# Seven block products for the last matrix product of an attention and two-layer expert kernel

## The chip, the cores and the metric

The kernel runs on one core of one Trainium2 chip. A core has TensorE (matmuls; PE in the profile, its weight loads PEld), VectorE (DVE), ScalarE (ACT), GpSimd (POOL) and SyncE (SP), which here issues all DMAs. Matmuls write to PSUM, eight banks of 512 fp32 numbers on each of 128 partitions; GpSimd can't read it. The metric is the device time of one execution in microseconds, lower is better. Inputs and outputs are fp32.

## The reference

```python
# attention with a small memory: q, k, v (8, 8, 576, 64), phi (8, 8, 576, 32)
a = softmax(phi, axis=2)
k_m = einsum('bhsm,bhsd->bhmd', a, k); v_m = einsum('bhsm,bhsd->bhmd', a, v)
attn = softmax(q @ k_m.T / sqrt(64)) @ v_m
x = attn.transpose(0, 2, 1, 3).reshape(4608, 512)
# first layer, d_ff 768
h = maximum(maximum(x @ w1, x @ w2), x @ w3)
x = h @ w_out                                   # 768 -> 512
# second layer, d_ff 1536
gate = 1 / (1 + exp(-(x @ w_gate)))             # 512 -> 1536
out = (gate * (x @ w_val)) @ w_out              # 1536 -> 512
```

The change concerns the last line alone: `gg = gate * val`, 4608 x 1536, times the second `w_out`, 1536 x 512.

## The kernel before

The program is written with a tile framework. It traces the instructions in the order of the Python code; a scheduler with a model of the engines then orders each engine's queue, and sets the waits. It may move instructions past one another, on TensorE and on SP as well, unless an instruction is pinned with `tc.keep_in_program_order`. Tiles come from pools: a tag with `bufs=n` has n buffers, and a new tile waits for the last reader of the tile that had its buffer.

**Precision.** A product of fp32 matrices is made of three matmuls in the type fp32r. `w_split` (L133) makes two parts of a matrix: ACT casts it to the high part, then GpSimd or VectorE subtracts that from the whole to get the low part (`sub`, L72). `PASSES` (L333) lists low x high, high x low, high x high, summed in PSUM.

**First half** (to about 559 us): attention, and the first layer in four passes of 1152 tokens (`h_step` L362, `x2_step` L389). Its output x goes to HBM as `x2s`. In the last pass, beside `x2_step`, the first operands of the second half are made.

**Second half.** The 4608 tokens are cut into five chunks (`SUPER`), each of two halves of 512, 512, 512, 384 and 384 tokens. In each chunk, six rounds j = 0..5 take 256 of the 1536 columns of d_ff: the two blocks of 128 columns j and j+6. A round of one chunk:

- *Up products.* x (two halves of tokens by two halves of the 512 inputs) times the gate weights (v = 0) and the value weights (v = 1) is a 2 x 2 block product. It is made in seven block products (Winograd's form of Strassen's method) for eight: seven sums of blocks of x (`XA`, made by `x_sums` and `x_split` once a chunk), seven of the weights (`TB`, made in the first chunk by `t_make`, kept in HBM as `tbs` and loaded by `t_load` from then on). `ORDER` = 1, 6, 2, 7, 5, 4, 3 is the order of the products. `up` (L734) makes one for one v: `product` (L691), six matmuls of 512 columns (384 in the small chunks), 14 ups a round.
- *Blocks.* `up` then joins the products to blocks (token half c, column block h). Products accumulate in the PSUM tags px, pz and pv, two banks each; ACT copies product 1 (L746), VectorE makes the sums u (L749). `block_done` (L712) makes a block: for v = 0 the sum (VectorE, L719) and the sigmoid (ACT, L721), for v = 1 the sum (L726) and the product with the sigmoid (L727, or L729 straight from PSUM). Then gg is split: cast on ACT (L731), difference on GpSimd (L732, which the profile shows under the helper's line 73). Block (0,0) comes after product 2, (1,1) after 5, (1,0) after 4, (0,1) after 3.
- *Down products.* `down` (L759) multiplies a row block of 128 tokens with the two blocks of `w_out` of this round: six matmuls of 512 columns into a bank of tag po (two banks). The accumulators `acc` lie in SBUF: ACT copies the first round's sum (L774), VectorE adds the others (L777). Down products of round j stand between the up products of round j+1, from the third up on. After the last round of a chunk the rows go to `out`.

`w_out` is split by `wo_make` in the first chunk, kept as `wos`, and loaded by `wo_load` later. Its tiles and those of TB share 11 buffers (`NQ`). The gate, value and w_out weights come as tiles `tw` by `tw_load` from `wbf`, those of round 0 into the 11 buffers, the later ones into three buffers of the pool `b2`, which takes the place of the first half's pool `low`.

When the next chunk's x is due (`x_load` in the fifth round), GpSimd makes its sums and ACT and GpSimd its seven splits in the sixth round.

Of the kernel before, what the change touches and what calls it, by code (L numbers as in the profile page):

```python
# [1 line left out]

# [16 lines left out]
def attn_moe_kernel(  # L19
# [443 lines left out]
    def t_make(j, pr):  # L463
# [13 lines left out]
        TB[0, j, pr] = kept(src, tbs[j, pr - 1], "tb", vec if pr in (2, 5) else pool)  # L477

    def wo_make(j):
        for h, i in enumerate((j, j + NJ)):  # L480
            WO[0, j, h] = kept(TW[j, 2][:, h], wos[i], "wo2", vec if h else pool)
# [5 lines left out]
    def wo_load(sc, j):  # L487
        for h in range(2):
            t = WO[sc, j, h] = q4_tile("wo2")
            dma(f32(t), wos[j + h * NJ])  # L490
# [220 lines left out]

    def block_done(sc, j, v, c, h, ps, other):  # L712
# [18 lines left out]
        act.copy(t[:, 0, :half], gf)  # L731
        sub(pool, t[:, 1, :half], gf, f32(t[:, 0, :half]))  # L732

    def up(sc, j, pr, v):  # L734
# [12 lines left out]
        elif pr in (6, 7):  # L747
            u = E["u", pr, v] = small(f"u{pr}", 2)[:, :half]
            vec.tensor_tensor(out=u, in0=ps[:, :half], in1=E["p1", v], op=ALU.add)  # L749
# [130 lines left out]
```

## Time and profile before

| | us |
|---|---|
| median of 3 runs | 1387.36 (1386.55 to 1387.68) |
| the profiled execution | 1387.49 |
| its span, first to last instruction | 1385.4 |
| mean granted clock of TensorE | 0.988 |
| down matmuls (L765), 1296 | 327.8 busy |
| evictions of the down products on VectorE (L777), 180 | 124.3 busy |
| differences of gg on GpSimd, 120 | 143.4 busy |

The page gives busy time, share and number of instructions of each engine, then the span in slices (a digit is a tenth; PEclk is the clock granted to TensorE). The view by stretches has one row for each stretch of time: its length, then busy us and number of instructions of PE, PEld, DVE, ACT and POOL, the granted clock, the DMA share and GB/s. The view by order in time has start, length, engine, line, operation, tiles, shape and count of merged instructions; brackets name idle time before them and what ended it. The view by line and shape has count, busy us, mean ns, idle us before and what ended it. The name px stands for all buffers of that tag.

### The profile page before, as it was taken

Reading aid. Unit: us, or ns where it says so; the run is one execution under the profiler, and the core shown is the slowest. Engines: PE = TensorE matmul, PEld = TensorE weight load, DVE = VectorE, ACT = ScalarE, POOL = GpSimd, SP = SyncE. Lnnn points to the kernel's source line nnn. Section 1 sums busy time; section 2 is a strip of 40 time slices with the busy share of each in tenths; the row PEclk is TensorE's granted clock in tenths of the full one; section 3 lists DMA queues with packets and bytes.
Section 4 is the critical chain, followed back from the end, with each engine's and each line's share of the span. In section 5 each row is a group of like instructions: output and inputs, shape, how many; then the busy total and the mean of one; then the engine's idle time right before and its main releaser. Section 6 shows DMA issues by size and latency. Waiting matters only on the chain.

```text
span 1385.4 us, 22143 instructions
## 1 busy us (share of the span) xinstructions
PE 1337.5 (97%) x7864; PEld 1183.9 (85%) x7864; DVE 863.1 (62%) x1533; ACT 576.3 (42%) x1220; POOL 514.6 (37%) x454
## 2 busy tenths in 40 slices
PE   6688999999999999999999999999999999999998
PEld 3578899999999989788888888888888899999997
DVE  5999759966975895566765344453445444554454
ACT  5687546645654664453343321233222322233221
POOL 2775422422331227553586111461112712161111
PEclk9899999999999999999999999999999999999999
DMA  9588757776757745965556544465454666566651
GB/s 314 178 273 304 265 171 262 238 236 225 235 165 261 240 131 170 336 243 198 198 198 228 183 166 153 167 205 190 159 178 167 210 228 222 198 227 237 211 202 72
DMA packets 112269, 292.43 MB, mean 211 GB/s; under 512 B 12576, under 2 KB 28960, under 8 KB 112160
## 3 DMA queue, kind: packets, MB, share of 16 engines
q1 hardware_dynamic: 112160, 291.03, 61.9%
q8 instruction: 62, 1.02, 0.3%
q14 instruction: 47, 0.39, 0.1%
HBM read 224.92 MB, written 66.06 MB: 210 GB/s over the span
## 4 chain that ended last, share of the span: by engine, by line
PE 79%; DVE 10%; DMA 4%; issue 2%; ACT 2%; POOL 1%; SPq 1%; DVEq 0%; ACTq 0%; POOLq 0%
PE po L765 21%; PE px L698 15%; PE pv L698 10%; PE pz L698 10%; PE ps L393 9%; PE ps L370 8%; DVE g L73 2%; PE ps L343 2%; PE ps L209 1%; PE ps L246 1%; DVE ca L129 1%; DVE ca L128 1%; DMA raw<-wb_dram 1%; DVE hm L382 1%; DVE hm L381 1%
## 5 line engine op out<-in xcount | busy, mean ns | idle before, releaser
L765 PE MATMUL po<-wo,gg 128*128 128x512 f32 x1296 | 327.8, 392 | 1.0 <-POOL gg L73 1.0
L73 POOL TENSOR_TENSOR gg<-gf,gg 128x512 fp32r<-128x512 f32 (+1 forms) x120 | 143.4, 1195 | 469.1 <-ACT gg L731 426.3
L765 PEld LDWEIGHTS po<-wo,gg 128*128 128x128 f32 x1296 | 242.4, 188 | 49.5 <-POOL gg L73 1.3
L370 PE MATMUL ps<-attn,g 128*128 128x288 f32 x1728 | 258.7, 302 | 21.0 <-DVE g L73 11.0
L370 PEld LDWEIGHTS ps<-attn,g 128*128 128x128 f32 x1728 | 244.7, 193 | 31.8 <-DVE hm L381 8.7
L698 PE MATMUL px<-xa,tb 128*128 128x512 f32 (+1 forms) x1080 | 244.1, 368 | 1.6 <-DVE gf L729 1.1
L777 DVE TENSOR_TENSOR acc<-po,acc 128x512 f32<-128x512 f32 x180 | 124.3, 691 | 176.0 <-PE po L765 175.8
L698 PEld LDWEIGHTS px<-xa,tb 128*128 128x128 f32 x1080 | 198.0, 188 | 30.4 <-DVE gf L729 1.6
L698 PE MATMUL pz<-xa,tb 128*128 128x512 f32 (+1 forms) x720 | 169.5, 368 | 1.8 <-DVE u L749 1.8
L698 PE MATMUL pv<-xa,tb 128*128 128x512 f32 (+1 forms) x720 | 170.4, 369 | 0.0
L73 POOL TENSOR_TENSOR h<-hm,h 128x288 fp32r<-128x288 f32 x96 | 82.7, 864 | 211.8 <-DVE h L70 111.3
L393 PE MATMUL ps<-h,wo 128*128 128x288 f32 x1152 | 158.5, 296 | 0.0
L393 PEld LDWEIGHTS ps<-h,wo 128*128 128x128 f32 x1152 | 154.3, 188 | 2.8 <-issue 2.6
L698 PEld LDWEIGHTS pz<-xa,tb 128*128 128x128 f32 x720 | 132.2, 188 | 20.9 <-issue 2.2
L698 PEld LDWEIGHTS pv<-xa,tb 128*128 128x128 f32 x720 | 132.8, 189 | 18.1
L731 ACT CAST gg<-gf 128x512 fp32r<-128x512 f32 (+1 forms) x120 | 69.4, 578 | 176.3 <-DVE gf L727 130.5
L749 DVE TENSOR_TENSOR u<-pz,p 128x512 f32<-128x512 f32 (+1 forms) x120 | 76.2, 635 | 97.9 <-PE pz L698 93.4
L73 DVE TENSOR_TENSOR g<-ps,g 64x384 fp32r<-64x384 f32 x180 | 99.4, 552 | 31.8 <-ACT g L357 28.8
L721 ACT ACTIVATE sg<-sg 128x512 f32<-128x512 f32 (+1 forms) x90 | 53.1, 590 | 145.4 <-DVE sg L719 145.1
L357 ACT CAST g<-ps 64x384 fp32r<-64x384 f32 x192 | 90.7, 473 | 36.4 <-DVE g L73 22.4
L73 POOL TENSOR_TENSOR xa<-xf,xa 128x512 fp32r<-128x512 f32 (+1 forms) x64 | 78.8, 1252 | 21.6 <-ACT xa L134 21.6
L727 DVE TENSOR_TENSOR gf<-gf,sg 128x512 f32<-128x512 f32 (+1 forms) x90 | 70.9, 788 | 10.9 <-ACT sg L721 1.3
(92 smaller groups left out, 1394.4 us busy)
## 6 DMA issues: line engine op xcount, KB each, us to landing
tb<-tbs SPq DMA_DIRECT2D x168, 512.0 KB, 3.8
wx<-wxs SPq DMA_DIRECT2D x72, 384.0 KB, 3.9
wo<-wos SPq DMA_DIRECT2D x48, 512.0 KB, 5.4
tbs<-tb SPq DMA_DIRECT2D x42, 512.0 KB, 2.9
raw<-wb_dram SPq DMA_DIRECT2D x48, 384.0 KB, 3.5
kv<-kvm_dram SPq DMA_DIRECT2D x48, 256.0 KB, 5.3
raw<-wx_dram SPq DMA_DIRECT2D x24, 384.0 KB, 3.8
wxs<-wx SPq DMA_DIRECT2D x24, 384.0 KB, 4.4
```

The costliest lines, as they stand in the source:

```text
L73: eng.tensor_tensor(out=o, in0=a, in1=b, op=ALU.subtract)
L343: pe.matmul(ps[:, :384], lhsT=vt[:, x, 2 * e:2 * e + 2].rearrange("p a m -> p (a m)"), rhs=w[:, y], start=(n == 0), stop=(n == 2),)
L357: act.copy(t[r, 0], ps[r, :384])
L370: pe.matmul(ps[w][:, :U], lhsT=G[b, j, g][:, x, 128 * w:128 * w + 128], rhs=at[:, y, hf * U:hf * U + U], start=(n == 0), stop=(n == 5),)
L393: pe.matmul(ps[:, :U], lhsT=wo1_t[:, x, (d * J + j) * 128:(d * J + j) * 128 + 128], rhs=H[u, j][:, y], start=(n == 0), stop=(n == 3 * J - 1),)
L698: pe.matmul(ps[:, :half], lhsT=w[:, a, o:o + 128], rhs=x[:, k, c, :half], start=(first and n == 0), stop=(n == 5), skip_group_check=not first,
L721: act.activation(out=sg, in_=src, func=AF.Sigmoid)
L727: vec.tensor_tensor(out=gf, in0=gf, in1=sg, op=ALU.mult)
L731: act.copy(t[:, 0, :half], gf)
L749: vec.tensor_tensor(out=u, in0=ps[:, :half], in1=E["p1", v], op=ALU.add)
L765: pe.matmul(ps, lhsT=GG[sc, j, c, h][:, x, 128 * m:128 * m + 128], rhs=WO[sc, j, h][:, y], start=(n == 0), stop=(n == 5),)
L777: vec.tensor_tensor(out=t, in0=ps, in1=t, op=ALU.add)
```

## The change

From the second chunk on, the product of gg and `w_out` is made in seven block products too. gg of a round is 2 x 2 blocks (c, h); the round's part of `w_out` is 2 x 2 blocks (h, half of the 512 outputs). The seven left sides are gg's blocks 1: (0,0), 2: (0,1), 4: (1,1) and sums 3, 5, 6, 7, made on VectorE in `block_done`; each is split as a block was, so there are seven splits a round for four. The seven right sides are made in the first chunk, which itself still uses eight products (`down0`, the old `down`), by `wo_make`, six steps a round, and kept in `wos`.

`down` makes a product for two row blocks at a time: six matmuls of 256 columns (three where a half has a third row block alone) into one bank, evicted at once. The seven products are accumulated each for itself over the six rounds; after the sixth `add` joins them to the four output blocks, on GpSimd and VectorE, all on VectorE in the last chunk. A down product follows each up product, from the first on. Products 1 and 4 come first, then those that are made late. `InOrder` pins every matmul of the second half behind the one traced before it.

```diff
+    class InOrder:
+
+        def __init__(self, eng):
+            self.eng = eng
+
+        def __getattr__(self, name):
+            fn = getattr(self.eng, name)
+            return lambda *a, **k: tc.keep_in_program_order(fn(*a, **k))
...
-    wos = tc.dram_tile([NI, 128, 2, DM], F32, name="wos")
+    wos = tc.dram_tile([NI // 2, 7, 128, 2, DM // 2], F32, name="wos")
...
-    NQ = 11
+    NQ = 7
     ORDER = (1, 6, 2, 7, 5, 4, 3)
+    DORDER = (1, 4, 6, 7, 5, 2, 3)
+    LORDER = (1, 6, 7, 5, 4, 2, 3)
+    HD = DM // 2
...
         for h, i in enumerate((j, j + NJ)):
-            t = TW[j, h] = tile()
+            t = TW[j, h] = b1.tile([128, 2, DM], F32, tag="tw", name="tw", bufs=2)
             dma(t.rearrange("p h c -> p (h c)"), wbf[i, :, 0:2 * DM])
-        t = TW[j, 2] = tile()
+
+    def wv_load(j):
+        t = TW[j, 2] = b2.tile([128, 2, DM], F32, tag="wv", name="wv", bufs=1)
...
+    def wo_load(sc, j, n):
+
+        order = dorder(sc, j)[2 * n:2 * n + 2]
+        t = wo_tile().rearrange("p a (h d) -> p h a d", h=2)
+        for h, pr in enumerate(order):
+            WO[sc, j, pr] = t[:, h]
+            dma(f32(t[:, h]), wos[j, pr - 1])
...
+    pe = InOrder(nc.tensor)
...
+    def gg_split(sc, j, pr, x):
+        half = SUPER[sc][1]
+        t = GG[sc, j, pr] = b2.tile([128, 2, 512], F32R, tag="gg", name="gg", bufs=8)
+        w_split(x, t[:, 0, :half], t[:, 1, :half])
...
+        elif (c, h) == (1, 0):
+            A11, A22 = F[0, 0], F[1, 1]
+            vec.tensor_tensor(out=A22, in0=gf, in1=A22, op=ALU.add)
+            sub(vec, gf, A11, gf)
+            sub(vec, A11, A22, A11)
+            for pr, x in ((6, A11), (7, gf), (5, A22)):
+                gg_split(sc, j, pr, x)
+        else:
+            gg_split(sc, j, 2, gf)
+            sub(vec, gf, gf, F[0, 0])
+            gg_split(sc, j, 3, gf)
...
+    def add(sc, x, y):
+        n = SUPER[sc][1] // 128
+        a, b = ACC[sc, x][:, :n], ACC[sc, y][:, :n]
+        (vec if x in (3, 5) or sc == LAST[0] else pool).tensor_tensor(out=a, in0=a, in1=b, op=ALU.add)
+
+    BLOCK = {2: (0, 0), 3: (0, 1), 4: (1, 0), 5: (1, 1)}
...
+    BEFORE = {1: ((2, 1),), 7: ((7, 6), (4, 7)), 6: ((6, 1),), 5: ((3, 5), (3, 6), (5, 7))}
+
+    def bank_of(sc, j, n):
+        tag = "po" if (sc, j) != LAST else ("po", "px", "pz", "pv")[n // 2 % 4]
+        return psB.tile([128, 512], F32, tag=tag, name=tag, bufs=2)
...
+    def down(sc, j, pr, q):
+        n = SUPER[sc][1] // 128
+        m0, m1 = 2 * q, min(2 * q + 2, n)
+        at = 2 * dorder(sc, j).index(pr) + q
+        ps = bank_of(sc, j, at).rearrange("p (m d) -> p m d", m=2)
+        for m in range(m0, m1):
+            for k, (x, y) in enumerate(PASSES):
+                pe.matmul(
+                    ps[:, m - m0],
+                    lhsT=GG[sc, j, pr][:, x, 128 * m:128 * m + 128],
+                    rhs=WO[sc, j, pr][:, y],
+                    start=(k == 0), stop=(k == 2),
+                )
+        if j == 0 and q == 0:
+            ACC[sc, pr] = acc_tile()
+        summed(j, ACC[sc, pr][:, m0:m1], ps[:, :m1 - m0])
...
+        if j == NJ - 1:
+            for x, y in BEFORE.get(pr, ()):
+                add(sc, x, y)
...
+        if (sc, j) != LAST and (at % 4 == 3 or at == 13):
+            wo_load(*after(sc, j), at // 4)
...
-                    if slot >= 3 and downs:
-                        down(*downs.pop(0))
+                    if downs and slot >= downs[0][0]:
+                        downs.pop(0)[1]()
...
+                x = [(pr, q) for pr in dorder(sc, j) for q in range(2)]
+                downs = [(n + 1, partial(down, sc, j, *a)) for n, a in enumerate(x)]
```

Other edits that go with it:

- `LORDER` is the order of the last round of all, whose bank comes from all four PSUM tags in turn.
- The sums of the next chunk's x move from the sixth round to the fourth (from the third chunk's x on), and half of the seven splits of x (those of products 6, 7 and 4) have their differences on VectorE, where GpSimd had all.
- The weights `tw` of all rounds lie in two buffers of the pool `b1`, the w_out weights (`wv`) in one buffer of `b2`; `wo_make` of round 0 moves from the end of the first half into the first round. Tiles of TB have the seven buffers alone, `w_out` has four of its own.
- The tile of product 7's sum u takes the buffer of p1; gg has 8 buffers for 6; the accumulators are seven tiles of 1024 numbers for eight of 512; `x2` has a pool of its own.

More of the change, by code (lines that the diff above doesn't have):

```diff
@@ L1 @@
 from contextlib import ExitStack
+from functools import partial
 import concourse.bass as bass
@@ L476, in t_make, with wo_tile, wo_make @@
             src = TD.pop(pr)
[L477 to L481, printed above, removed]
+        TB[0, j, pr] = kept(q4_tile("tb"), src, tbs[j, pr - 1], vec if pr in (2, 5) else pool)
+    def wo_tile():
+        return b2.tile([128, 2, DM], F32R, tag="wo2", name="wo2", bufs=4)
+    def wo_make(j, n):
+        w = TW[j, 2]
+        B11, B12, B21, B22 = w[:, 0, :HD], w[:, 0, HD:], w[:, 1, :HD], w[:, 1, HD:]
+        if n < 2:
+            t = WO[0, j, n] = wo_tile()
+            w_split(w[:, n], t[:, 0], t[:, 1], vec if n else pool)
+            for pr, c in (((1, 0),), ((2, 0), (3, HD)))[n]:
+                dma(wos[j, pr - 1], f32(t[:, :, c:c + HD]))
+            return
+        pr = (6, 7, 5, 4)[n - 2]
+        if pr == 6:
+            sub(vec, B11, B12, B11)
+            TD["w"] = b2.tile([128, HD], F32, tag="wd", name="wd", bufs=1)
+            sub(vec, TD["w"], B22, B11)
+        elif pr == 7:
+            sub(vec, B12, B22, B12)
+        elif pr == 4:
+            sub(vec, TD["w"], B21, TD["w"])
+        x = {5: B11, 7: B12}.get(pr)
+        t = b2.tile([128, 2, HD], F32R, tag="wt", name="wt", bufs=1)
+        kept(t, TD["w"] if x is None else x, wos[j, pr - 1], pool)
     def t_load(sc, j, pr):
@@ L485, in t_load, with dorder @@
         dma(f32(t), tbs[j, pr - 1])
[L487 to L490, printed above, removed]
+    def wo_load(sc, j, n):
[4 more added lines that the diff above has]
+            dma(f32(t[:, h]), wos[j, pr - 1])
+    def dorder(sc, j):
+        return LORDER if (sc, j) == LAST else DORDER
     XA = {}
@@ L653, in attn_moe_kernel @@
                 b1 = tc.alloc_tile_pool(name="b1", bufs=1, side="right", reuse_waits="tile")
+                xo = tc.alloc_tile_pool(name="xo", bufs=1, side="right")
             gens = []
@@ L722, in block_done @@
             return
-        gf = small("gf", 4)[:, :half]
+        gf = F[c, h] = small("gf", 4)[:, :half]
         sg = E.pop(("sg", c, h))
@@ L747, in up @@
         elif pr in (6, 7):
-            u = E["u", pr, v] = small(f"u{pr}", 2)[:, :half]
-            vec.tensor_tensor(out=u, in0=ps[:, :half], in1=E["p1", v], op=ALU.add)
+            p1 = E["p1", v]
+            u = E["u", pr, v] = p1 if pr == 7 else small("u6", 2)[:, :half]
+            vec.tensor_tensor(out=u, in0=ps[:, :half], in1=p1, op=ALU.add)
         elif pr == 2:
@@ L757, in up, with store, acc_tile, summed @@
             block_done(sc, j, v, 0, 1, ps, E["u", 6, v])
-    def down(sc, j, c, m):
-        t0, half = SUPER[sc]
-        ps = psB.tile([128, DM], F32, tag="po", name="po", bufs=2)
+    def add(sc, x, y):
[3 more added lines that the diff above has]
+    BLOCK = {2: (0, 0), 3: (0, 1), 4: (1, 0), 5: (1, 1)}
+    def store(sc, pr, m0, m1):
+        t0, half = SUPER[sc]
+        c, d = BLOCK[pr]
+        r0 = t0 + c * half
+        dma(out[r0 + 128 * m0:r0 + 128 * m1, d * HD:d * HD + HD].rearrange("(m p) d -> p m d", p=128),
+            ACC[sc, pr][:, m0:m1])
+    BEFORE = {1: ((2, 1),), 7: ((7, 6), (4, 7)), 6: ((6, 1),), 5: ((3, 5), (3, 6), (5, 7))}
+    def bank_of(sc, j, n):
+        tag = "po" if (sc, j) != LAST else ("po", "px", "pz", "pv")[n // 2 % 4]
+        return psB.tile([128, 512], F32, tag=tag, name=tag, bufs=2)
+    def acc_tile():
+        return b2.tile([128, 4, HD], F32, tag="acc", name="acc", bufs=7)
+    def summed(j, t, ps):
+        if j == 0:
+            act.copy(t, ps)
+        else:
+            vec.tensor_tensor(out=t, in0=ps, in1=t, op=ALU.add)
+    def down0(sc, j, c, m):
+        half = SUPER[sc][1]
+        ps = bank_of(sc, j, 0)
         n = 0
```

77 lines of the change are left out of this document (45 added, 32 removed).

## The prediction, made before the run

> **What bounds the kernel now.** The page was read first, then busy time by stretches, then the order in time on TensorE.
>
> ```profile
> span 1385.4 us, 22143 instructions
> PE 1337.5 (97%) x7864; PEld 1183.9 (85%) x7864; DVE 863.1 (62%) x1533; ACT 576.3 (42%) x1220; POOL 514.6 (37%) x454
> PEclk9899999999999999999999999999999999999999
> ```
> ```profile
> 559.10:585.60 26.50, 23.07 (x93) 18.03 (x92) 15.22 (x19) 11.58 (x22) 13.62 (x10) 0.94 0.88 323
> ...
> 800.00:900.00 100.00, 100.00 (x441) 82.55 (x440) 48.27 (x73) 22.63 (x38) 25.63 (x20) 1.00 0.46 158
> ...
> 1100.00:1200.00 100.00, 100.00 (x521) 92.76 (x520) 46.14 (x79) 24.38 (x48) 20.74 (x21) 1.00 0.64 221
> ```
>
> In the second half (from 559 us, the part that the change touches) TensorE is busy without a hole, at the full clock, while VectorE is busy for less than half of it (48.27 and 46.14 of 100 us) and the DMA engines for 46 to 64%. Only the first round of it (559 to 586 us) has holes. A busy matmul row is not matmul work at its peak, so the next view is the pitch, from one start to the next:
>
> ```profile
> 914.39 2.88 PE L698 MATMUL px<-xa,tb 128*128 128x512 f32 x12
> 917.11 2.88 PE L698 MATMUL pz<-xa,tb 128*128 128x512 f32 x12
> ...
> 922.09 2.91 PE L765 MATMUL po<-wo,gg 128*128 128x512 f32 x12
> 924.84 1.52 PE L698 MATMUL px<-xa,tb 128*128 128x512 f32 x6
> ```
> ```profile
> 1264.65 2.27 PE L698 MATMUL px<-xa,tb 128*128 128x384 f32 x12
> 1266.75 0.86 PE L698 MATMUL pz<-xa,tb 128*128 128x384 f32 x4
> ```
> ```profile
> 544.74 14.58 PE L393 MATMUL ps<-h,wo 128*128 128x288 f32 x109
> 559.16 2.92 PE L698 MATMUL px<-xa,tb 128*128 128x512 f32 x12
> ```
> ```profile
> 251.67 0.60 PE L195 MATMUL ps<-ident,et 128*128 128x128 f32 x4
> 252.10 0.27 PE L196 MATMUL ps<-ident,et 128*64 128x128 f32 x1
> ```
>
> 512 columns: 2.72 us / 12 = 227 ns in the up products and 2.75 / 12 = 229 ns in the down products (L765). 384 columns: 2.10 / 12 = 175. 288 columns: 14.42 / 109 = 132. Transposes of 128 columns: 0.43 / 4 = 108. Every one loads 128x128 weights of its own. From 288 to 512 columns the pitch grows by 95 ns over 224 columns, 0.42 ns each. So TensorE bounds this half, and what counts there is columns with a small fixed part per matmul.
>
> **The change, part by part.**
>
> *1. Down products.* A round is one value of j, 256 columns of d_ff; a chunk of halves of 512 tokens has 4 row blocks in each half, one of 384 has 3. Now a round has 2 x 4 x 6 = 48 matmuls of 512 columns (36 in the small chunks). After the change it has 7 x 4 x 3 = 84 of 256 (63). No row has 256 columns. The line through 288 and 512 gives 132 - 32 x 0.42 = 119 ns. Bounds: 132 (it can't be dearer than the wider 288) and 108 (transposes with the same weight load). I take 119, next to the 288 row. A large round: 84 x 119 = 10.00 us for 48 x 229 = 10.99. A small one: 7.50 for 8.24. Rounds whose down products run beside the next round's up products: 12 large, 11 small. 12 x 0.99 + 11 x 0.74 = **20.1 us less**. These are 12 x 84 + 11 x 63 = 1701 matmuls, so a pitch of 132 adds 22.1 us and one of 108 takes off 18.7 more.
>
> The Trainium skill (TensorE: Matmul & The Clock Gate, "Back-to-back issue gap") gives N/2.4 + 2.5 ns for a warm matmul alone, 109 ns at 256 columns. By it the sum would be 17 us lower; but it gives 216 ns at 512 columns, where this trace has 227, so the line through the rows stands.
>
> *2. The last round.* Its down products stand alone after the last up product.
>
> ```profile
> 1369.89 2.24 PE L698 MATMUL pv<-xa,tb 128*128 128x384 f32 x12
> ...
> 1373.13 8.53 PE L765 MATMUL po<-wo,gg 128*128 128x512 f32 x36 [1.00 <-POOL gg L73]
> ...
> 1381.69 0.69 DVE L777 TENSOR_TENSOR acc<-po,acc 128x512 f32<-128x512 f32 x1 [0.68 <-PE po L765]
> ```
> ```profile
> L777 DVE TENSOR_TENSOR acc<-po,acc 128x512 f32<-128x512 f32 x180 | 124.3, 691 | 176.0 <-PE po L765 175.8
> ...
> L749 DVE TENSOR_TENSOR u<-pz,p 128x384 f32<-128x384 f32 x48 | 26.7, 556 | 35.2 <-PE pz L698 33.4 <-ACT p L746 1.8
> ```
>
> Now: from the end of the last up product (1369.89 + 2.24 = 1372.1) to the last eviction (1382.4) 10.3 us, set by TensorE. After: 7 evictions of 512 elements at 0.69, 7 of 256, and 7 sums of 768, all on VectorE in the last chunk. From 384 (556 ns) and 512 (691) an element costs 1.05 ns, so 256 take 0.42 us and 768 take 0.96. 7 x 0.69 + 7 x 0.42 + 7 x 0.96 = 14.5 us; with the last block's add, product and difference (3 x 0.56), one eviction left over (0.42) and about 1 us of gaps, 17.6 us. TensorE would need some 9. **VectorE sets the tail: 7.3 us more** (5 to 9).
>
> *3. Work beside TensorE.* Three more casts on ACT, three more differences on POOL, four sums on VectorE and 14 evictions for 8, each round.
>
> ```profile
> L73 POOL TENSOR_TENSOR gg<-gf,gg 128x512 fp32r<-128x512 f32 x72 | 94.7, 1315 | 267.8 <-ACT gg L731 224.9 <-PE po L765 40.9 <-DMA tw<-wbf 1.9
> L731 ACT CAST gg<-gf 128x512 fp32r<-128x512 f32 x72 | 44.8, 622 | 106.2 <-DVE gf L727 75.4 <-DVE gf L729 29.2 <-PE po L765 1.5
> tb<-tbs SPq DMA_DIRECT2D x168, 512.0 KB, 3.8
> ```
>
> POOL: 7 x 1.32 = 9.2 of 29 us; ACT: 1.9 us more; both are hidden, since the first operand that is made late (product 6, after up product 4) is used seven steps of 2.1 us later. Were that cover gone, each would cost up to its 1.9 us. Of DMA, w_out goes from 1.0 to 1.75 MB a round (14 issues for 2 on SP's queue, counting halves); a load has most of a 22 to 29 us round and takes about 4 to land (3.8 for tb), so I cost it at nothing. The queue for tb has 7 buffers for 11, but each load is still issued a round ahead. VectorE: 14 x 0.69 + 10 x 0.69 (reads of PSUM in the blocks) + 0.69 + 7 x 0.69 + about 0.8 of gaps = 22.9 of 29.1 us, 79%. Not the bound in a mean round.
>
> *4. TensorE's order fixed.* A matmul that waits now holds up everything behind it, and evictions are what it can wait for: the down products have two PSUM banks, so a bank must be free 4.15 us after its matmuls ended (two ups of 1.36, two downs of 0.71).
>
> ```profile
> 933.74 0.69 DVE L726 TENSOR_TENSOR gf<-pv,u 128x512 f32<-128x512 f32 x1 [0.21 <-PE pv L698]
> 934.53 0.69 DVE L727 TENSOR_TENSOR gf<-gf,sg 128x512 f32<-128x512 f32 x1
> 935.14 0.68 DVE L719 TENSOR_TENSOR sg<-px,u 128x512 f32<-128x512 f32 x1
> ```
> ```profile
> 704.47 0.69 DVE L726 TENSOR_TENSOR gf<-pv,u 128x512 f32<-128x512 f32 x1 [0.29 <-PE pv L698]
> 705.80 1.31 DVE L73 TENSOR_TENSOR wo<-tw,wo 128x512 fp32r<-128x512 f32 x1 [0.64 <-ACT wo L134]
> 707.03 1.77 DVE L727 TENSOR_TENSOR gf<-gf,sg 128x512 f32<-128x512 f32 x1
> ```
> ```profile
> L727 DVE TENSOR_TENSOR gf<-gf,sg x90: 557/692/1843, 581.4 to 1372.9; 128x512 f32<-128x512 f32 x54, 128x384 f32<-128x384 f32 x36
> ```
>
> After up product 4 VectorE has add, product and three sums in a row. A dependent step takes 0.79 us (933.74 to 934.53), an independent one 0.61. If the eviction traced behind them waits for all: 0.3 + 4 x 0.79 + 0.61 + 0.69 = 4.8 us, counted from the up product's end, where TensorE wants the bank after 4.15: 0.6 us lost, in 16 rounds 10 us. In the round after each of three chunk changes three sums of 1024 elements (1.23 each) come on top, about 3.3 us each time, 10 in all; in the round before, six differences for the next x, 1.5 us each time, 4.5 in all. Together **0 to 25 us**. But the second fence shows an instruction that the program gives later (the w_out difference) put between two dependent ones. Where evictions slip in so, a bank is late by one instruction, within the slack. I take 4.
>
> *5. The entry.*
>
> ```profile
> 570.78 0.62 ACT L134 CAST tb<-tw 128x512 fp32r<-128x512 f32 x1 [8.08 <-DMA tw<-wbf]
> ...
> 585.68 2.88 PE L698 MATMUL px<-xa,tb 128*128 128x512 f32 x12
> ```
>
> The first round takes 585.68 - 559.16 = 26.5 us for 84 x 227 ns = 19.1: 7.4 lost, behind a load of gate weights that ACT waits for. That load now goes to buffers that exist earlier, but w_out's comes in its place, and the order can't bend round a wait. Between 7 less and 4 more; I take 2 less.
>
> Sum: -20.1 + 7.3 + 4 - 2 = -10.8. The profiled execution took 1387.49 us, 2.1 more than its span of 1385.4, and the median is 1387.36, the same within 0.01%. 1387.4 - 10.8 = **1376.6 us**; its own range 1371 to 1382.
>
> **Rivals.**
>
> *VectorE's queue holds up TensorE* (slower). The strict order of part 4 holds: 25 us of stalls for 4, 1387.4 - 20.1 + 7.3 + 25 - 2 = 1397.6. It decides once evictions end more than 4.15 us after their matmuls. For: the fixed order, 79% load, and L727 at 1843 ns where it usually takes 692, which POOL's longer hours make commoner. Against: the slipped instruction. At 13 us of stalls it comes to 1385.6, no difference.
>
> The Trainium skill (SBUF — State Buffer, "Who interferes with whom") says that a VectorE instruction with two SBUF inputs and a GpSimd one that reads SBUF exclude each other for the whole instruction. L727's 1843 ns agrees; the new sums are all of that kind.
>
> *Narrow matmuls don't get cheaper*: 256 columns at 132 ns, as the 288 row. 22.1 us more than forecast: 1398.7. Against: 108 ns was reached with the same weight load.
>
> *All of it comes through*: no stalls and 6 us won at the entry, 1387.4 - 20.1 + 7.3 - 6 = 1368.6. For: TensorE never waits between 600 and 1372 us now.
>
> *Pitch at the lower bound*, 108 ns: 18.7 less than forecast, 1358.
>
> **How the numbers follow.** Forecast 0.50; VectorE's queue 0.16, half-way (no difference) 0.10; narrow matmuls 0.06; all of it 0.15; lower pitch 0.03. A measurement of this kernel tells 0.2% (2.8 us) from no change. Faster: 0.50 + 0.15 + 0.03 = 0.68. Same: 0.10. Slower: 0.22. The range takes in the forecast, half-way, most of "all of it", most of VectorE's queue and the nearer side of the narrow matmuls: 1364 to 1399.
>
> **What would show it.** Step 1: down matmuls at a pitch of 119 ns. Step 2: VectorE without idle time from the last up product on, TensorE done some 8 us earlier than it. Step 4: TensorE's idle time put down to the eviction of po, at most 0.3 us a round. Step 5: the first round of chunk one, 19 to 26 us. A pitch above 130 ns, or 20 us of waits for po, makes the prediction wrong.

## The result, and the profile after

| | before | after |
|---|---|---|
| median of the runs, us | 1387.24 | 1401.90 (1401.55 to 1402.63, 4 runs) |
| ratio, 95% interval | | 1.0111 [1.0099, 1.0123] |
| span of the profiled execution, us | 1385.4 | 1399.9 |
| start of the second half, us | 559.2 | 558.6 |
| chunks 0 to 4, us | 175.1, 180.2, 180.2, 140.1, 137.4 | 182.8, 176.9, 180.7, 144.7, 134.7 |
| last up product to the end of the span, us | 13.2 | 21.6 |

The change makes the kernel 1.1% slower; 1376.6 us had been forecast. A chunk here lasts from the start of its first up product to the start of the next chunk's; round (c, j) is round j of chunk c, cut after every 84 up matmuls (before, the scheduler mixes neighbouring rounds). The page after:

```profile
span 1399.9 us, 24589 instructions
PE 1328.9 (95%) x8620; PEld 1204.9 (86%) x8620; DVE 1048.1 (75%) x1833; ACT 624.4 (45%) x1344; POOL 629.1 (45%) x538
```

TensorE is busy for 8.6 us less than before, yet the span is 14.5 us longer: its work did shrink, but the time around it grew by more. VectorE has 185 us more to do, GpSimd 115. Busy time by rounds of after, (0,2), (2,0), (2,4), (3,0), (3,3) and (4,0), shows where the waits are (columns: length, then PE, PEld, DVE, ACT, POOL, clock, DMA share, GB/s), and below it one round of before:

```profile
615.97:648.47 32.50, 30.84 (x134) 24.62 (x133) 25.71 (x35) 13.28 (x26) 20.75 (x16) 1.00 0.72 251
...
918.25:953.13 34.88, 30.48 (x170) 25.33 (x169) 28.47 (x37) 8.73 (x16) 26.37 (x17) 1.00 0.63 195
1040.63:1069.80 29.17, 29.17 (x170) 25.72 (x169) 21.08 (x33) 7.51 (x13) 9.21 (x7) 1.00 0.60 190
1098.97:1131.14 32.17, 26.72 (x171) 24.88 (x169) 29.47 (x38) 8.06 (x16) 25.12 (x16) 0.97 0.73 224
1177.29:1199.32 22.03, 22.03 (x149) 22.03 (x148) 16.47 (x33) 6.01 (x13) 6.99 (x7) 1.00 0.80 255
1243.67:1268.37 24.70, 23.26 (x150) 21.79 (x148) 20.72 (x36) 6.93 (x15) 16.79 (x13) 1.00 0.76 245
```
```profile
644.15:674.17 30.02, 30.02 (x133) 24.78 (x132) 21.45 (x29) 10.36 (x19) 11.10 (x10) 1.00 0.56 207
```

Rounds (2,4) and (3,3) have no hole: 29.17 us for 30.02 before, and 22.03 for 22.88. That is the gain, 12 x 0.86 + 11 x 0.85 = 19.7 us. Rounds right after a chunk change lose it again: (2,0) lasts 5.7 us more than 29.17; (3,0), which has the small chunk's 84 ups at 173 ns and the large chunk's 84 downs at 118, 24.4 together, loses 7.7. There GpSimd is busy for 26 and 25 us, in a steady round for 9.

```profile
1040.63 1.55 PE L60 MATMUL px<-xa,tb 128*128 128x512 f32 x6
1042.02 0.87 PE L60 MATMUL po<-wo,gg 128*128 128x256 f32 x6
1042.73 1.52 PE L60 MATMUL px<-xa,tb 128*128 128x512 f32 x6
```

In time order on TensorE in (2,4): six matmuls of 256 columns in 0.71 us, 118 ns each. The order in time of after around the wait in (2,0), GpSimd first, then TensorE, with the wait in brackets:

```profile
925.88 2.34 POOL L83 TENSOR_TENSOR xf<-xf 128x384 f32<-128x384 f32 x2
928.17 2.40 POOL L828 TENSOR_TENSOR acc<-acc 128x1024 f32<-128x1024 f32 x1
930.52 5.03 POOL L83 TENSOR_TENSOR gg<-gf,gg 128x512 fp32r<-128x512 f32 x4
```
```profile
931.84 0.97 PE L60 MATMUL po<-wo,gg 128*128 128x256 f32 x6 [1.77 <-POOL gg L83]
```

Two differences of x and a join (L828) stand on GpSimd before the split of gg that TensorE needs. The differences (128 x 384) are of chunk 3; the program gives them in round (2,4), the fifth of chunk 2 (not the fourth, as the list above has it), and the scheduler took them forward. Three other waits of this round are for evictions; of the first, VectorE, then TensorE:

```profile
916.56 1.50 DVE L778 TENSOR_TENSOR gf<-gf,sg 128x512 f32<-128x512 f32 x1
917.98 1.50 DVE L83 TENSOR_TENSOR xa<-xf,xa 128x512 fp32r<-128x512 f32 x1
...
920.00 0.68 DVE L853 TENSOR_TENSOR acc<-po,acc 128x512 f32<-128x512 f32 x1
```
```profile
920.78 0.95 PE L60 MATMUL po<-wo,gg 128*128 128x256 f32 x6 [1.01 <-issue]
```

The profile names no releaser ("issue"), but TensorE starts 0.10 us after the eviction at 920.00 has ended, and so it is with all six such waits of the second half. The view of waits for the whole second half (who waited for whom: us in total, times, the longest) then reads, for the down products into tag po:

```profile
PE po L60 <- DVE acc L853: 6.8, 6, 3.4
PE po L60 <- POOL gg L83: 4.6, 7, 1.8
PE po L60 <- issue: 3.6, 6, 1.0
```

So 10.4 us of these waits are for late evictions on VectorE, 4.6 us for late splits on GpSimd, and none is for a transfer. In (3,0) it is the joins, on VectorE and on GpSimd, that make the eviction late:

```profile
1114.05 2.80 DVE L83 TENSOR_TENSOR gf<-gf 128x512 f32<-128x512 f32 x1
...
1121.26 2.37 DVE L828 TENSOR_TENSOR acc<-acc 128x1024 f32<-128x1024 f32 x1
...
1124.62 4.42 DVE L828 TENSOR_TENSOR acc<-acc 128x1024 f32<-128x1024 f32 x2
1128.96 0.68 DVE L853 TENSOR_TENSOR acc<-po,acc 128x512 f32<-128x512 f32 x1
```
```profile
1113.87 2.43 POOL L828 TENSOR_TENSOR acc<-acc 128x1024 f32<-128x1024 f32 x1
...
1124.44 2.37 POOL L828 TENSOR_TENSOR acc<-acc 128x1024 f32<-128x1024 f32 x1
```
```profile
1129.69 1.65 PE L60 MATMUL po<-wo,gg 128*128 128x256 f32 x6 [3.36 <-DVE acc L853]
```

A difference that takes 0.68 us elsewhere (the middle one of 36) takes 2.80 beside GpSimd's 2.43 us join, and two joins in a row (4.42 us) hold back the eviction at 1128.96, for which TensorE waits 3.36 us. In the first chunk the four differences of w_out do the same (order in time of after, VectorE, then TensorE; 0.41 us is the shortest such difference):

```profile
621.55 1.51 DVE L83 TENSOR_TENSOR wv<-wv 128x256 f32<-128x256 f32 x1
623.09 1.40 DVE L83 TENSOR_TENSOR wd<-wv 128x256 f32<-128x256 f32 x1
624.41 1.52 DVE L83 TENSOR_TENSOR wv<-wv 128x256 f32<-128x256 f32 x1
...
626.45 0.67 DVE L853 TENSOR_TENSOR acc<-po,acc 128x512 f32<-128x512 f32 x1
```
```profile
627.18 1.66 PE L60 MATMUL po<-wo,gg 128*128 128x512 f32 x6 [1.45 <-DVE acc L853]
```

The wait of 3.36 us costs more than itself. Round (3,1) has no hole, and still lasts 2.1 us more than 22.03:

```profile
1131.14:1155.27 24.13, 24.13 (x149) 24.13 (x148) 11.69 (x23) 11.89 (x27) 6.94 (x7) 0.90 0.77 252
1128.90:1135.73 6.83, 6.04 (x23) 6.04 (x24) 5.29 (x11) 1.59 (x3) 0.00 (x0) 0.50 0.99 349
```

The granted clock is 0.50 for 6.83 us from about the end of the wait on: two down and two up products take 6.34 us (1129.69 to 1136.03) where at the pitches above they take 3.5. That is 2.8 us. In the 20 traces of this case, between the first and the last up product, the clock was at half within 3.4 us after the end of all 28 waits of TensorE of 3.07 us or more, of 22 of the 36 between 1.7 and 3.07 us, and of one of the 57 between 1.0 and 1.7 us.

And the tail, the last lines of TensorE and of VectorE:

```profile
1388.85 1.33 PE L60 MATMUL pz<-wo,gg 128*128 128x256 f32 x9 [0.66 <-POOL gg L83]
```
```profile
1389.54 1.01 DVE L853 TENSOR_TENSOR acc<-px,acc 128x512 f32<-128x512 f32 x2
1390.47 3.55 DVE L828 TENSOR_TENSOR acc<-acc 128x768 f32<-128x768 f32 x4
1393.94 1.01 DVE L853 TENSOR_TENSOR acc<-po,acc 128x512 f32<-128x512 f32 x2
1394.87 1.00 DVE L853 TENSOR_TENSOR acc<-pz,acc 128x512 f32<-128x512 f32 x2
```

TensorE ends at 1390.2, VectorE at 1395.9, 17.6 us after the last up product (1378.3).

The account, after against before: down products -19.7; first chunk +7.7; waits at (1,0), (2,0), (3,0) and (4,0) and small ones, with the 2.8 us of half clock in (3,0) and (3,1), +19.3; tail +8.4; start -0.6. Together +15.1, where the spans differ by 14.5.

### The profile page after: what moved, and what is told of

It reads as the page before. It is cut to its first block, busy times and chain, and to the rows that moved or that the text cites. A ratio compares the mean times of both kernels' runs of the same rounds, so it can differ in the third digit from the quotient of the medians.

```text
span 1399.9 us, 24589 instructions
## 1 busy us (share of the span) xinstructions
PE 1328.9 (95%) x8620; PEld 1204.9 (86%) x8620; DVE 1048.1 (75%) x1833; ACT 624.4 (45%) x1344; POOL 629.1 (45%) x538
## 4 chain that ended last, share of the span: by engine, by line
PE 46%; DVE 5%; POOL 4%; issue 3%; DMA 2%; ACT 1%; DVEq 0%; SPq 0%; ACTq 0%; POOLq 0%
PE po L60 16%; PE px L60 12%; PE pz L60 9%; PE pv L60 8%; DMA wos<-wt 1%; DVE acc L853 1%; POOL gg L83 1%; DVE acc L828 1%; DVE gf L778 1%; POOL wt L83 1%; POOL tb L83 1%; POOL xf L83 1%; DVE gf L777 0%; DMA tb<-tbs 0%; DVE sg L770 0%
## 5 line engine op out<-in xcount | busy, mean ns | idle before, releaser
L83 POOL TENSOR_TENSOR gg<-gf,gg 128x512 fp32r<-128x512 f32 (+1 forms) x192 | 230.3, 1217 | 348.9 <-ACT gg L144 283.8
L60 PE MATMUL po<-wo,gg 128*128 128x256 f32 (+1 forms) x2007 | 333.5, 299 | 15.3 <-DVE acc L853 6.8
L60 PEld LDWEIGHTS po<-wo,gg 128*128 128x128 f32 x2007 | 300.1, 190 | 47.5 <-DVE acc L853 9.7
L380 PE MATMUL ps<-attn,g 128*128 128x288 f32 x1728 | 258.1, 302 | 20.1 <-DVE g L83 11.1
L60 PE MATMUL px<-xa,tb 128*128 128x512 f32 (+1 forms) x1080 | 252.1, 371 | 0.1
L853 DVE TENSOR_TENSOR acc<-po,acc 128x512 f32<-128x512 f32 (+1 forms) x310 | 195.2, 630 | 59.4 <-PE po L60 57.5
L60 PEld LDWEIGHTS px<-xa,tb 128*128 128x128 f32 x1080 | 190.6, 189 | 21.9 <-ACT p L811 0.5
L144 ACT CAST gg<-gf 128x512 fp32r<-128x512 f32 (+1 forms) x192 | 103.5, 573 | 167.7 <-DVE gf L83 70.2
L60 PEld LDWEIGHTS pv<-xa,tb 128*128 128x128 f32 x720 | 126.1, 188 | 14.2
L353 PE MATMUL ps<-wx,vt 128*128 128x384 f32 x288 | 70.5, 354 | 3.6 <-DVE hm L392 1.1
L83 POOL TENSOR_TENSOR xa<-xf,xa 128x512 fp32r<-128x512 f32 (+1 forms) x40 | 53.9, 1367 | 21.0 <-ACT xa L144 21.0
```

Source lines behind the costliest of these rows:

```text
L60: return lambda *a, **k: tc.keep_in_program_order(fn(*a, **k))
L83: eng.tensor_tensor(out=o, in0=a, in1=b, op=ALU.subtract)
L144: act.copy(hi, w)
L353: pe.matmul(ps[:, :384], lhsT=vt[:, x, 2 * e:2 * e + 2].rearrange("p a m -> p (a m)"), rhs=w[:, y], start=(n == 0), stop=(n == 2),)
L380: pe.matmul(ps[w][:, :U], lhsT=G[b, j, g][:, x, 128 * w:128 * w + 128], rhs=at[:, y, hf * U:hf * U + U], start=(n == 0), stop=(n == 5),)
L853: vec.tensor_tensor(out=t, in0=ps, in1=t, op=ALU.add)
```

## The experiments

Each kernel ran beside the one before on the same chip; ratios are to it (after: 1.0111). One profile of each gives the rounds. The diffs show the main lines of each edit; dots stand for lines left out. How far two executions differ: the second half starts at 555.7 to 560.9 us, whatever the edit; seven kernels with the first chunk of after take 181.7 to 184.1 us for it; and seven with the same code around (2,0) take 34.8 to 36.4 us for that round: three have 34.8 to 34.9 at a granted clock of 1.00, four 36.2 to 36.4 at 0.95, after the same wait of some 1.77 us.

**The fixed order.** `e1_unpinned`, after without it:

```diff
-    pe = InOrder(nc.tensor)
+    pe = nc.tensor
```


> The changed kernel with TensorE's order left to the scheduler, nothing else. Theory A (the fixed order turns lateness of other engines into stalls, in the first chunk and at chunk changes): most of the 8 us lost in the first chunk and of the 18 lost at the chunk changes comes back, 1378 to 1388 us. Theory B (VectorE and GpSimd have too much to do there, whatever TensorE's order): within 4 us of the changed kernel, 1398 to 1406.

1427.47 us, 1.0305 [1.0286, 1.0323]: 25 us slower than with the order. The scheduler now puts two downs behind one another, which then wait for the bank, and 24 us of downs are left after the last up, where the longest wait is for their weights (TensorE in order of time):

```profile
1158.26 2.93 PE L885 MATMUL po<-wo,gg 128*128 128x256 f32 x12 [3.88 <-DVE acc L853]
...
1411.71 1.31 PE L885 MATMUL px<-wo,gg 128*128 128x256 f32 x9 [2.73 <-DMA wo<-wos]
```

`e2_before_pinned`, the kernel before with its second half's order fixed:

```diff
+    pe = InOrder(nc.tensor)
```


> The kernel before with every matmul of its second half pinned in the traced order, nothing else. Theory A: the first chunk alone gets slower by about 8 us, 1393 to 1398 us. Theory B: the order costs nothing by itself, 1385 to 1390.

1397.62 us, 1.0087 [1.0072, 1.0102]. Nearly all of it is lost at chunk changes, and the steady rounds keep their 30.03 us (22.94 for 22.88 in the small chunks):

```profile
709.06 1.65 PE L59 MATMUL po<-wo,gg 128*128 128x512 f32 x6 [2.38 <-POOL gg L82]
...
741.87 2.92 PE L59 MATMUL po<-wo,gg 128*128 128x512 f32 x6 [2.50 <-POOL gg L82]
```

So a strict order does cost about 12 us in the old scheme, where a scheduler can bend round a late split; in the new one it is worth 25. Giving it up as a whole is no cure. Whether after would lose less at chunk changes with an order that is free there alone was not tried.

**The joins.** `e4_no_joins` leaves those of chunks 1 to 3 out:

```diff
-            for x, y in BEFORE.get(pr, ()):
-                add(sc, x, y)
+            if sc == LAST[0]:
+                for x, y in BEFORE.get(pr, ()):
+                    add(sc, x, y)
```


> The changed kernel without the joins of the seven accumulators (add) in chunks 1 to 3, so that their outputs are not joined; the last chunk's joins and all stores remain. Theory B: the three rounds after a chunk change lose 18 us mostly to the joins, 12 to 16 us come back, 1386 to 1390. If the other work there does it (splits and sums of the next x): less than 5 us, 1397 to 1402.

1388.96 us, 1.0025 [1.0014, 1.0036]: 12 to 13 us less than after. (2,0) takes 31.11 us, (3,0) 26.56, (3,1) 22.03, (4,0) 22.67: 3.8, 5.6, 2.1 and 2.0 less, 13.5 together. Busy time in (2,0) and (3,0) of this kernel:

```profile
919.00:950.11 31.11, 29.67 (x171) 25.56 (x170) 25.66 (x38) 9.26 (x16) 16.28 (x13) 1.00 0.72 230
1095.93:1122.49 26.56, 25.37 (x170) 24.46 (x169) 22.39 (x37) 8.10 (x16) 14.46 (x12) 1.00 0.80 249
```

GpSimd has 10 us less to do there. The joins are the largest part of the loss at chunk changes, not all of it. Without them no wait of (3,0) is over 1 us and the clock stays at 1.00 there and in (3,1), so the 2.8 us of half clock are among what came back.

`e7_joins_later` leaves them in, but takes VectorE's three out of the round after the chunk change:

```diff
-                add(sc, x, y)
+                if pr == 5 and sc != LAST[0]:
+                    LATER.append(partial(join_later, sc, x, y, {(3, 6): 3, (5, 7): 5}.get((x, y))))
+                else:
+                    add(sc, x, y)
...
+                    if LATER and j == 1:
+                        LATER.pop(0)()
```


> The changed kernel with VectorE's three joins of a chunk moved to the second round after the chunk change, where ACT does the evictions and VectorE is busy for 16 of 29 us, and GpSimd's first join moved behind product 6; no work is left out. Theory B1: most of the 13.5 us that the joins cost comes back, 8 to 12, 1390 to 1394 us. Theory B2 (GpSimd's four joins and what they hold up cost it): 2 to 5 us, 1397 to 1400.

1395.75 us, 1.0072 [1.0053, 1.0091]: 5 to 6 us less. (3,0) falls from 32.2 to 26.84 us, near the 26.56 without joins; (2,0), whose longest wait is still for a split on GpSimd, stays at 34.75 (0.95 of the clock), and the rounds that got the joins, (2,1) and (3,1), take 30.07 and 24.81.

`e13_joins_behind_gg` keeps GpSimd's joins behind its splits of gg:

```diff
-        w_split(x, t[:, 0, :half], t[:, 1, :half])
+        w_split(x, t[:, 0, :half], t[:, 1, :half], InOrder(pool) if sc else None)
...
-        (vec if x in (3, 5) or sc == LAST[0] else pool).tensor_tensor(out=a, in0=a, in1=b, op=ALU.add)
+        (vec if x in (3, 5) or sc == LAST[0] else InOrder(pool)).tensor_tensor(out=a, in0=a, in1=b, op=ALU.add)
```


> GpSimd's joins and its splits of gg keep the program's order among each other, so that no join of 2.4 us can run ahead of a split that TensorE waits for; nothing is left out. Theory 1 (the place of the joins): the rounds (2,0) and (4,0) lose 1 to 3 us less each, the whole takes 1396 to 1400 us. Theory 2 (their length beside VectorE's work, wherever they stand, or VectorE's own joins): the rounds stay as they are, the whole 1400 to 1403 us.

1402.27 us, 1.0113 [1.0097, 1.0130], as after: (3,0) wins 2.5 us, (2,0) takes 37.1 (at a clock of 0.95). The place of GpSimd's joins alone brings nothing.

**The next chunk's x.** `e6_xsplit_gpsimd` gives all its splits to GpSimd, `e9_sums_in_order` keeps GpSimd's sums of it, from the third chunk's x on, in the program's order:

```diff
-                        x_split(sc + 1, pr, vec if n % 2 else None)
+                        x_split(sc + 1, pr)
```


> The changed kernel with the differences of all seven splits of x on GpSimd, as before the change. Theory B1 (VectorE's queue is what is late at a chunk change): 2 to 5 us come back of the 4.6 that are lost there without the joins, 1397 to 1400. Theory B2 (GpSimd is as late): it gets slower by 2 to 6 us, 1404 to 1408.

1402.12 us, 1.0115 [1.0090, 1.0140]: (2,0) 2.0 us shorter, (1,0) 2.6 longer. No difference.

```diff
-        pool.tensor_tensor(out=r[1, k], in0=r[21, k], in1=r[22, k], op=ALU.add)
+        pinned = InOrder(pool) if sc > 1 else pool
+        pinned.tensor_tensor(out=r[1, k], in0=r[21, k], in1=r[22, k], op=ALU.add)
...
```


> The sums and differences of x that GpSimd makes for a chunk two or more ahead are kept in the program's order on GpSimd, so that they cannot run ahead of the splits of gg; nothing is left out. Theory 1 (GpSimd's early work delays the splits of gg in the rounds after the chunk change): round (2,0), 34.9 us after the change, loses 2 to 4 us and the whole becomes 1398 to 1400 us. Theory 2 (GpSimd's queue is simply too full there, in any order: the joins of 2.4 us are what delays): the round keeps 34 to 35 us, the whole stays within 1401 to 1403 us.

1396.56 us, 1.0075 [1.0060, 1.0090]: 5 us less, a little more than the first theory's 2 to 4. (2,0) falls to 32.25, (3,0) to 29.26, (3,1) to 22.04; the longest wait of (3,0) is 2.4 us now and the clock stays at 1.00, so the gain holds those 2.8 us too. On GpSimd in (2,0) the sums are gone from ahead of the splits, which now start at 926.69, 9.7 us into the round; in after it was 12.3:

```profile
924.31 2.41 POOL L829 TENSOR_TENSOR acc<-acc 128x1024 f32<-128x1024 f32 x1 [2.43 <-DVE acc L854]
926.69 5.03 POOL L83 TENSOR_TENSOR gg<-gf,gg 128x512 fp32r<-128x512 f32 x4
```

**The first chunk.** `e3_wt_rotates` gives the new right sides more buffers, since ACT's casts into the single one wait for a store (27.4 us in all):

```diff
+        if j < NJ - 2:
+            t = b1.tile([128, 512], F32R, tag="xf", name="wt", bufs=8).rearrange("p (a c) -> p a c", a=2)
...
```


> The changed kernel with the four sums of w_out's blocks in rounds 0 to 3 of the first chunk written to one of eight idle buffers of the pool b1 in place of the one buffer wt, so that ACT's cast need not wait for the store of the sum before. Theory C (ACT waits 27 us in all for these stores and holds up the casts and sigmoids behind): the first chunk is 3 to 6 us shorter, 1396 to 1399 us. Theories A and B: the wait is not on the path, 1400 to 1404.

1402.92 us, 1.0122 [1.0105, 1.0139], first chunk 183.8: the wait falls from 27.4 to 8.7 us and the chunk is no shorter, so it is off the path. `e5_no_w_sums` stores the first block in place of four of the seven right sides:

```diff
+        dma(wos[j, pr - 1], f32(WO[0, j, 0][:, :, :HD]))
+        return
         if pr == 6:
```


> The changed kernel without making the right sides of products 4, 5, 6 and 7 in the first chunk: their casts, differences and sums are left out (some 1.6 us of ACT, 3 of GpSimd and 2 to 6 of VectorE a round), the first block is stored in their places, so the output of chunks 2 to 5 is not the product. Theory B: the first chunk's loss of 8 us is this work, on VectorE above all, where differences with two SBUF inputs take up to 1.5 us for 0.4; 5 to 7 us come back, 1395 to 1397. If the loss comes from the smaller sets of buffers (7 for 11, one for wv): less than 2 us, 1400 to 1403.

1398.49 us, 1.0086 [1.0065, 1.0107]. Rounds (0,1) to (0,5) take 30.30 to 30.45 us, 4.5 us less together than in after; the first round is no shorter (27.4 for 26.6). So this work costs 4 to 5 us; the whole kernel is 3.5 us faster. Three kernels then moved it. `e10_wout_gpsimd`, the four differences to GpSimd, and a difference for the next round's product 6 pinned on VectorE:

```diff
-            TD[5] = less(B12, B11)
+            TD[5] = less(B12, B11, InOrder(vec) if j == 1 else vec)
...
-            sub(vec, B11, B12, B11)
+            sub(pool, B11, B12, B11)
...
```


> The four differences of w_out in the first chunk's rounds are made by GpSimd instead of VectorE, and the difference that the right side of the next round needs is kept in the program's order on VectorE, so that it no longer stands behind one that waits for a transfer; nothing is left out. Theory 1 (the first chunk loses its 8 us to VectorE, which stands in a queue behind a transfer in round 1 and is slowed by GpSimd in the others): the first chunk becomes 3 to 8 us shorter, the whole 1394 to 1399 us. Theory 2 (GpSimd is the late one there, since VectorE's evictions wait for the splits of gg): more work on GpSimd makes the first chunk 2 to 6 us longer, the whole 1404 to 1408 us.

1405.19 us, 1.0145 [1.0130, 1.0160]: the first round falls to 22.1 us, but (0,2) takes 35.96 (the granted clock was 0.95 there) and the chunk 183.7; 1.6 of the 3 us by which its profile is longer than after's lie ahead of the second half. `e11_td_in_order`, the pin alone:

```diff
-            TD[5] = less(B12, B11)
+            TD[5] = less(B12, B11, InOrder(vec) if j == 1 else vec)
```


> The difference of the up weights that the right side of the second round's product 6 needs is kept in the program's order on VectorE; nothing is left out. Theory 1 (in the first round TensorE waits 5.4 us for a sum of VectorE that stands behind a difference whose transfer has not landed): the first round falls from 26.6 to 22 or 23 us and the whole to 1396 to 1399 us. Theory 2 (the round before it or the transfers set the entry): the time of the round moves to its neighbours, the whole stays within 1400 to 1403 us.

1402.23 us, 1.0118 [1.0101, 1.0135]: the first round 28.5. Product 6's sum is in time, and TensorE waits later in the same round for VectorE, which has the w_out differences and weight splits in between: the second theory. TensorE's longest wait of that round, first in after, then in this kernel:

```profile
572.67 4.52 PE L60 MATMUL pz<-xa,tb 128*128 128x512 f32 x12 [5.26 <-DVE u L815]
```
```profile
582.80 5.30 PE L60 MATMUL pv<-xa,tb 128*128 128x512 f32 x12 [3.94 <-DVE sg L770]
```

`e12_wsums_spread`, the four differences in the program's order on VectorE:

```diff
-            sub(vec, B11, B12, B11)
+            sub(InOrder(vec), B11, B12, B11)
...
```


> The four differences of w_out in each round of the first chunk are kept in the program's order on VectorE, so that they stand one after each of four up products and not back to back; nothing is left out. Theory 1 (they stop TensorE's evictions because they run in a row, 6 us of VectorE beside GpSimd): rounds 2 to 5 of the first chunk fall to about 30.3 us and the whole by 3 to 4 us, to 1398 us. Theory 2 (their sum counts, or GpSimd's share of the work does): the first chunk keeps its 183 us, the whole stays within 1400 to 1404 us.

1404.91 us, 1.0138 [1.0118, 1.0158]: (0,2) 34.5, (0,4) 34.1, worse, not better. Now an eviction stands behind a difference of the up weights, itself not one of the four, that waits for its transfer:

```profile
629.61 0.69 DVE L83 TENSOR_TENSOR td<-tw 128x512 f32<-128x512 f32 x1 [5.22 <-DMA tw<-wbf]
...
632.23 0.68 DVE L853 TENSOR_TENSOR acc<-po,acc 128x512 f32<-128x512 f32 x1
```

**The tail.** `e8_last_round_eight` makes the last round in eight products, and the last chunk's joins one round earlier, four of the seven on GpSimd:

```diff
-        if sc == 0:
+        if sc == 0 or (sc, j) == LAST:
             gg_split(sc, j, (c, h), gf)
...
-        if j == NJ - 1:
+        if j == (NJ - 1 if sc != LAST[0] else NJ - 2):
...
```


> The changed kernel with the last round of the last chunk in eight products, as before the change, and the last chunk's joins moved ahead of it, beside that round's up products. Step 2 of the prediction (VectorE's evictions and joins set the tail): the tail goes from 21.6 back to 13 to 14 us; with up to 1 us lost in the round before, 1394 to 1396 us. If the tail were set by the late operands of products 6, 7 and 3: 1399 to 1402.

1397.65 us, 1.0078 [1.0056, 1.0100]; the tail 19.0 us for 21.6, less than expected: three joins of VectorE at 1374 to 1378 us now delay the last blocks, TensorE waits 3.0 us for a split, and the clock is at half for 6.83 us after that: the first 12 matmuls take 5.3 us for 2.7.

**Together.** `c2_joins_tail_x` joins e7, e8 (with VectorE's three joins behind the last up product) and e9, and gives the later chunks' x splits to GpSimd alone (its expectation, and those of c4 and c5, have this the wrong way round):

```diff
-                        x_split(sc + 1, pr, vec if n % 2 else None)
+                        x_split(sc + 1, pr, vec if n % 2 and sc == 0 else None)
...
+    for x, y in ((3, 5), (5, 7), (3, 6)):
+        add(LAST[0], x, y)
...
```


> Three edits together: VectorE's joins are spread over the following round; the last round of the last chunk is made in eight products, with the last chunk's three joins of VectorE behind its last up product; the splits of x for the later chunks leave GpSimd, whose sums of x are kept in order. Nothing is left out. If their single effects add up (6 us from the joins, 4 to 8 us from the tail, 2 us from the order on GpSimd), the whole takes 1386 to 1391 us; if they fight for VectorE's time in the same rounds, 1392 to 1398 us.

1385.33 us, 0.9999 [0.9986, 1.0011]: level with the kernel before. That is what the single effects add up to (5.4, 4.6 and 5.0 us), though otherwise shared out: the tail alone gives 8.7. The tail is 12.9 us at full clock, chunks 3 and 4 take 136.5 and 135.7. (2,0) 32.05 and (3,0) 25.23 us:

```profile
916.75:948.80 32.05, 29.79 (x170) 25.50 (x169) 26.23 (x34) 8.31 (x15) 27.48 (x17) 1.00 0.66 214
1095.46:1120.69 25.23, 24.98 (x170) 24.47 (x169) 22.73 (x32) 6.95 (x15) 21.51 (x14) 1.00 0.71 225
```

`c3_all` adds e10 to it, `c4_all_in_order` adds e11, e12 and e13:

> The three edits of the combination before and the two in the first chunk. If the first chunk's loss comes from VectorE, 3 to 8 us less than that combination: 1380 to 1387 us, level with the kernel before or faster. If GpSimd is the late one in the first chunk, 2 to 6 us more than it.

> The combination of spread joins, eight products in the last round and x splits off GpSimd, which took 1385.3 us, with the three orders of the runs before it. If each gives what its first theory says (4, 3 and 3 us): 1375 to 1379 us, below the kernel before. If none does: 1385 us.

1388.16 us, 1.0016 [1.0006, 1.0026], and 1388.36 us, 1.0018 [1.0007, 1.0030]: neither helps; in c4 the first chunk takes 189.4 us and (1,5) 35.6. Last, `c5_wt_splits_vector` moves the right sides' splits to VectorE, `c6_more_splits_vector` also those of one side of the up weights (the last two lines):

```diff
-        kept(t, TD["w"] if x is None else x, wos[j, pr - 1], pool)
+        kept(t, TD["w"] if x is None else x, wos[j, pr - 1], vec)
...
-        TB[0, j, pr] = kept(q4_tile("tb"), src, tbs[j, pr - 1], vec if pr in (2, 5) else pool)
+        TB[0, j, pr] = kept(q4_tile("tb"), src, tbs[j, pr - 1], vec if pr in (2, 5, 4) else pool)
```


> The combination that took 1385.3 us (spread joins, eight products in the last round, x splits off GpSimd), with the four splits a round of the new right sides on VectorE instead of GpSimd; nothing is left out. Theory 1 (the sum of the time that VectorE and GpSimd hold against each other counts; a split of 128x256 takes VectorE 0.41 us, GpSimd 0.74 us and more): the first chunk falls from 183.5 to about 180 us, the whole to 1382 us. Theory 2 (VectorE's own queue is the late one in these rounds, so anything added to it costs): the first chunk grows to 185 to 188 us, the whole to 1387 to 1390 us.

> The same, and also the splits of the up weights' right side 4 on VectorE: 0.69 us instead of 1.30 us each, two a round. Theory 1: another 1 to 2 us less than the run before it, 1380 to 1382 us. Theory 2: another 2 us more, 1389 to 1392 us.

1387.60 us, 1.0010 [1.0000, 1.0019], first chunk 186.0; and 1385.26 us, 0.9994 [0.9984, 1.0004], 182.7. The first speaks for the second theory, the second for neither. No version beats the kernel before by more than a measurement tells.

## Why the prediction was wrong

*Step 1 held.* 118 ns at 256 columns against 119; 19.7 us against 20.1. The Trainium skill (TensorE: Matmul & The Clock Gate, "Back-to-back issue gap") has 109 ns by its formula for a matmul alone; the trace does not reach it.

*Step 2 held.* 17.6 us from the last up product to the last eviction, as worked out, and VectorE is busy for 16.6 of them; 8.4 us more to the end of the span against 7.3. TensorE is done 5.7 us before VectorE, not 8, since it waits 2.8 us for splits meanwhile. That the figure fits to the tenth is luck: three of the seven joins took 1.1 to 1.6 us beside GpSimd's splits where 0.96 had been reckoned, and evictions in a row less than 0.69 each.

*Step 4 failed, and most of the error is there:* stalls taken as 4 us were 19. The prediction had the mechanism, an eviction that stands late in VectorE's queue (10.4 us of TensorE's waits in the second half), and terms up to 25 us for it, and struck them out because of one instruction that slipped between two dependent ones. In steady rounds that was right: the 10 us reckoned for 16 rounds did not appear at all. Nor, but for 0.3 us in (3,5), did the 4.5 us reckoned for the rounds before a chunk change. In the rounds after one it was wrong: the 10 us reckoned there became 18. The joins make 12 to 13 of them (e4). The prediction named the right place, with too low a price: three sums at 1.23 us on VectorE, where GpSimd's four joins of 2.4 us slow them to as much as 3.28 and stand ahead of splits besides; the last of the next x's differences run over into the same round (917.98); and the half clock after a long wait, 2.8 us, is a cost that it has no term for.

*Step 3 failed there too.* It costed GpSimd at nothing from a steady round, 9 of 29 us, which the trace after confirms (9.21). At a chunk change the x sums, splits and joins bring it to 26, splits of gg are late, and VectorE's instructions beside it take longer: putting the sums back in order won 5 us (e9). "VectorE 79% in a mean round" hid the same thing: 72% in steady rounds, 82 to 92% in the bad ones.

*Step 5 failed with its sign.* 2 us less had been forecast for the first round, 24.5 for 26.5; it takes 26.6. Counted by up matmuls that is 1.8 more than before, where seven of the next round's were already made by then, and rounds (0,1) to (0,5) lose 5.9. The prediction had no term for that: it priced moving w_out's work, not the four further right sides a round. They cost 4 to 5 us (e5). The first round's wait moves with VectorE's queue (e10, e11).

The misses are 0.4, 1.1, 15 and 9 us (the start's 0.6 taken off the last), close to the 25.3 by which the time was missed. The rival nearest the outcome was VectorE's queue at 1397.6; it stopped TensorE, but only at chunk changes and in the first chunk, and with GpSimd's part in it: GpSimd's order (e9) and VectorE's joins (e7) were worth about 5 us each. The fixed order, which that rival made a condition, is worth 25 us to the new scheme (e1).

The Trainium skill (SBUF — State Buffer, "Who interferes with whom") says that a VectorE instruction with two operands in SBUF and a GpSimd one that reads SBUF shut each other out. 2.80 us for 0.68 beside a join of 2.43 agrees. Evictions, with one operand in PSUM, stay at 0.69 at most (all 310 of tag po): they come late by standing in the queue, not by being slowed.

Open: which part of the right sides' work makes the first chunk's 4 to 5 us. Moving it to GpSimd, spreading it and moving its splits to VectorE all failed to win it back; and c2 still spends 8 us more on that chunk than before, and 3 us more on each of (2,0) and (4,0) than a steady round takes. Why some waits of 1.7 to 3.07 us are followed by half clock and others are not is open too.

## What to carry to other kernels

A block scheme that saves matmul columns pays with additions on the other engines; price them in the stage where they fall together with other periodic work (chunk changes, first pass, tail), not in a mean round. Where two engines slow each other, cost an instruction by the longest time it shows beside the other engine, and don't strike out a bound because one row escaped it. Look at the granted clock after a wait of TensorE of some 2 us or more: the wait itself may not be all that it costs. What brought something here was spreading the joins over the next round, putting GpSimd's sums back in order, and the old product in the last round, about 5 us each; moving work from one of the two engines to the other brought nothing.

## What the runs showed that was not expected

- The same rule on TensorE, its order fixed, costs one kernel 12 us and saves another 25 (e2, e1). In the trace of e1 the loss is at down products that the scheduler put one behind the other, which wait for their bank, and at the end; that the order as traced fits the two banks is argued from this, not shown by itself.
- Pinning four differences on VectorE made the first chunk longer than the scheduler's order did: VectorE then stood for 5.2 us at a transfer, with evictions behind it (e12).
- Sums of 128 x 1024 take GpSimd 2.4 us; VectorE takes 1.21 us undisturbed, but up to 3.28 beside GpSimd, more than GpSimd itself.
- After a wait of TensorE of 3.07 us or more the granted clock was always at half for 3.41 or 6.83 us, after shorter ones down to 1.7 us in 22 of 36 cases. All of the spread of round (2,0), 34.8 to 36.4 us with the same code, goes with it.
